# Second layer's W_in products by Strassen's rule (seven block products for eight) in chunks of 768 tokens

## The chip, the cores and the metric

The kernel runs on one core of a Trainium2 chip. The metric is the time of one execution on the device in microseconds (us); the median of three runs of the kernel before is 1091.63 us (1090.07 to 1092.5).

## The reference

Three stages follow one another: causal attention mixed with a memory read, a gated layer, and a second layer. Only the second layer's first product is computed in another way; all values are fp32, the weights arrive as float64 bit patterns.

```python
def _moe_ref(x, w_gate, w_val, w_out):      # x: 2304 x 512, d_ff = 1536
    gate = 1.0 / (1.0 + np.exp(-(x @ w_gate)))
    val = x @ w_val
    return (gate * val @ w_out).astype(np.float32)

def _moe2_ref(x, w_in, w_out):              # x: 2304 x 512, d_ff = 2048
    h = x @ w_in
    relu6 = np.clip(h + 3.0, 0.0, 6.0)
    g = h * relu6 / 6.0
    return (g @ w_out).astype(np.float32)
```

## The kernel before, in words

Every fp32 product is made of three matmuls on fp32r halves: each operand is split into a high part (a ScalarE copy that rounds) and a low part (a VectorE subtraction), and high·high, high·low and low·high are summed in PSUM (`mm3`, L181 to L185; `split`, L177). A weight is loaded as float64 bits into a staging tile `wst` (pool of 2), turned into fp32 by a chain of seven VectorE and two ScalarE operations (`convert`, L141 to L157, on 512 columns at a time in the later phases) and kept in one of 18 slots `wslot`.

Phase A (attention, with the first part of the gated layer as filler) ends near 418 us. Phase B (`phase_b`, L599) finishes the gated layer: five chunks of tokens, the last four of 468, and for each chunk and each block f of 128 hidden units `g1` (24 matmuls, then tanh on ScalarE, a product and the split on VectorE) and one item later `g2` (12 matmuls into the accumulators). Beside it VectorE and ScalarE convert weights ahead of time (`w_next`). When a chunk ends, VectorE adds the accumulators to `xp` (L643) and SyncE's queue writes the result to `x2` in DRAM.

Phase C (`phase_c`, L660) is the second layer: six chunks of 384 tokens by 16 blocks f. `g3` (L667) makes 12 matmuls of 384 columns for one block of h, then ScalarE and VectorE make `r` and split it into `hs`; `g4` (L684) of the item before makes 9 matmuls of 512 columns into three accumulators. All 16 blocks of both weights stay on the chip. In phases B and C the order on every engine is the scheduler's, which places each instruction by a simulated time; in phase A, and in the changed phase C, the order on TensorE is the program's.

Of the kernel before, what the change touches and what calls it, by code (L numbers as in the profile page):

```python
# [23 lines left out]
CB = 384  # L24
# [34 lines left out]
WB = 468  # L59

# [15 lines left out]
class Kernel:  # L76
# [64 lines left out]
    def convert(self, sl, st):  # L141
# [4 lines left out]


# [8 lines left out]
        nc.vector.tensor_tensor(hif, hif, lof, op=ALU.add)
        nc.vector.tensor_tensor(sl[:, 1], hif, sl[:, 0].bitcast(F32), op=ALU.subtract)  # L157

    def w_convert(self):
# [3 lines left out]
        keys, st, pool = self.wstaged.pop(0)  # L163
        sl = pool.tile([128, 2, len(keys), 512], F32R, name="wslot", tag="wslot")
# [293 lines left out]
    def phase_a(self):  # L458
# [99 lines left out]
        keys += [[(2, f, 0), (2, f, 1)] for f in range(FF2)]  # L558
# [40 lines left out]
    def phase_b(self):  # L599
# [7 lines left out]
        def g1(ci, t0, n, f, first, last):  # L607
            if first:
                st["xs"] = self.split_x(st["x"], n)
                nx = CHB[ci + 1] if ci + 1 < len(CHB) else None  # L610
                st["x"] = self.load_x(self.xd, *nx) if nx else self.load_x(self.x2, 0, CB)
# [36 lines left out]
        prev = None  # L648
# [8 lines left out]
        self.x_next = st["x"]  # L657


    def phase_c(self):  # L660
        nc = self.nc
        NTK = CB // 128
        NC = NT // CB
        work = [(c, f) for c in range(NC) for f in range(FF2)]
        st = {"x": self.x_next}

        def g3(c, f):  # L667
            if f == 0:
                st["xs"] = self.split_x(st["x"], CB)
                if c + 1 < NC:  # L670
                    st["x"] = self.load_x(self.x2, (c + 1) * CB, CB)
            w = self.weight(2, f, 0)
            ps = self.ps_g.tile([128, 512], F32, name="g", tag="g")
            for k in range(KT):
                cc = slice(128 * k, 128 * k + 128)
                self.mm3(ps[:, :CB], (w[:, 0, cc], w[:, 1, cc]), st["xs"][k], k == 0, k == KT - 1)
            r = self.br.tile([128, WB], F32, name="th", tag="th", bufs=2)
            gs = self.br.tile([128, 2, WB], F32R, name="hs", tag="hs", bufs=3)
            nc.scalar.activation(r[:, :CB], ps[:, :CB], AF.Relu, bias=self.three)  # L679
            nc.vector.scalar_tensor_tensor(r[:, :CB], r[:, :CB], 6.0, ps[:, :CB], op0=ALU.min, op1=ALU.mult)  # L680
            self.split(gs[:, 0, :CB], gs[:, 1, :CB], r[:, :CB], nc.scalar, nc.vector)
            return gs

        def g4(gs, c, f):  # L684
            w = self.weight(2, f, 1)
            if f == 0:
                st["acc"] = [self.ps_a.tile([128, 512], F32, name="acc", tag="acc") for _ in range(NTK)]
            for m in range(NTK):
                cc = slice(128 * m, 128 * m + 128)
                a = st["acc"][m]  # L690
                nc.tensor.matmul(a, gs[:, 0, cc], w[:, 0, :], start=(f == 0), stop=False)  # L691
                nc.tensor.matmul(a, gs[:, 0, cc], w[:, 1, :], start=False, stop=False)  # L692
                nc.tensor.matmul(a, gs[:, 1, cc], w[:, 0, :], start=False, stop=(f == FF2 - 1))  # L693
                if f == FF2 - 1:
                    o = self.br.tile([128, 512], F32, name="xp", tag="xp", bufs=4)
                    nc.scalar.activation(o, a, AF.Copy, scale=1.0 / 6.0)
                    r0 = c * CB + 128 * m
                    nc.sync.dma_start(self.out[r0 : r0 + 128, :], o)

        prev = None  # L700
        for item in work:
            gs = g3(*item)
            if prev:
                g4(*prev)
            prev = (gs, *item)
            self.w_next()
        g4(*prev)
# [64 lines left out]
```

## Time and profile before

| | |
|---|---|
| runs | 1092.5, 1090.07, 1091.63 us (median 1091.63) |
| profiled execution, span from first to last instruction | 1089.9 us |
| TensorE busy | 1059.1 us (97%) |
| VectorE busy / ScalarE busy | 610.6 us (56%) / 513.7 us (47%) |
| phase B, 418.3 to 686.0 us | VectorE 208.47 us, ScalarE 104.63 us of 267.70 |
| phase C, 685.8 to 1085.4 us | VectorE 130.14 us, ScalarE 124.48 us of 399.60 |

The profile is of one execution. A matmul's row shows a modelled end, so consecutive matmuls overlap in the rows: their rate is read from the starts. Busy shares do not tell what a stage waits for; the waits before an engine's instructions do. Of the 1091.63 us of the median, 1.7 lie outside the profiled span.

### The profile page before, as it was taken

To read this page: it belongs to the slowest core of one execution; us is meant where nothing else is said; L and a number is where in the kernel's file an instruction comes from. 1 tells how busy PE (TensorE), PEld (TensorE's weight loads), DVE (VectorE), ACT (ScalarE), POOL (GpSimd) and SP (SyncE) were. 2 spreads that over 40 slices of the span, in tenths; PEclk is the share of its full clock that TensorE was granted. 3 is DMA by queue.
4 is the path that set the end of the run, shared out by engine and by line. 5 is a ranking of instruction groups with operands and counts; after the bars stand their busy time and mean duration, and the time that the engine had idled before them with its cause. 6 is when DMAs were issued, how large, how long until landed. Compare 5 with 4: busy or idle time off the path is not lost.

```text
span 1089.9 us, 16041 instructions
## 1 busy us (share of the span) xinstructions
PE 1059.1 (97%) x5968; PEld 915.3 (84%) x5968; DVE 610.6 (56%) x1484; ACT 513.7 (47%) x1123; POOL 59.6 (5%) x90
## 2 busy tenths in 40 slices
PE   5789999999999999999999999999999999999998
PEld 3458778878878899999888888999999989999997
DVE  7999885453455358888987158923232232322322
ACT  5989885566546644345433134423233232332322
POOL 3212211100110000000000000000000000000000
PEclk9879999999999999999999999999999999999999
DMA  6755642424242134335353142301001010000000
GB/s 215 217 176 171 205 124 73 134 83 121 63 121 78 63 126 131 116 116 181 124 176 103 43 157 99 103 1 58 1 19 40 1 58 1 30 29 1 30 1 30
DMA packets 56303, 98.55 MB, mean 90 GB/s; under 512 B 7328, under 2 KB 40608, under 8 KB 56224
## 3 DMA queue, kind: packets, MB, share of 16 engines
q1 hardware_dynamic: 56224, 97.52, 27.9%
q8 instruction: 47, 0.77, 0.3%
q14 instruction: 32, 0.26, 0.1%
HBM read 79.51 MB, written 17.99 MB: 89 GB/s over the span
## 4 chain that ended last, share of the span: by engine, by line
PE 90%; DVE 4%; DMA 2%; ACT 2%; issue 1%; SPq 1%; POOL 0%; ACTq 0%
PE g L185 12%; PE g L184 12%; PE g L183 12%; PE acc L691 6%; PE acc L692 6%; PE acc L693 6%; PE m L183 6%; PE m L184 5%; PE m L185 5%; PE t L352 4%; PE pv L376 4%; PE s L294 4%; PE acc L183 3%; PE acc L185 3%; PE acc L184 3%; DMA aux<-in_aux 2%
## 5 line engine op out<-in xcount | busy, mean ns | idle before, releaser
L184 PE MATMUL g<-xs,wslot 128*128 128x384 f32 (+2 forms) x672 | 235.4, 351 | 0.0
L185 PE MATMUL g<-xs,wslot 128*128 128x384 f32 (+2 forms) x672 | 235.1, 351 | 0.0
L183 PE MATMUL g<-xs,wslot 128*128 128x384 f32 (+2 forms) x672 | 231.2, 351 | 0.0
L680 DVE SCALAR_TENSOR_TENSOR th<-th,g 128x384 f32<-128x384 f32 x96 | 53.2, 554 | 220.1 <-ACT th L679 219.8
L679 ACT ACTIVATE th<-g,three 128x384 f32<-128x384 f32 x96 | 55.8, 582 | 219.9 <-PE g L185 219.1
L184 PEld LDWEIGHTS g<-xs,wslot 128*128 128x128 f32 x672 | 126.1, 188 | 9.2
L183 PEld LDWEIGHTS g<-xs,wslot 128*128 128x128 f32 x672 | 126.0, 188 | 8.8
L185 PEld LDWEIGHTS g<-xs,wslot 128*128 128x128 f32 x672 | 126.1, 188 | 6.8
L178 ACT CAST hs<-th 128x384 fp32r<-128x384 f32 (+2 forms) x132 | 70.0, 530 | 92.9 <-DVE th L680 49.6
L691 PE MATMUL acc<-wslot,hs 128*128 128x512 f32 x288 | 113.7, 395 | 0.0
L692 PE MATMUL acc<-wslot,hs 128*128 128x512 f32 x288 | 113.5, 394 | 0.0
L693 PE MATMUL acc<-wslot,hs 128*128 128x512 f32 x288 | 109.2, 394 | 0.0
L179 DVE TENSOR_TENSOR hs<-th,hs 128x384 fp32r<-128x384 f32 (+2 forms) x132 | 76.1, 577 | 50.0 <-ACT hs L178 49.4
L312 ACT ACTIVATE P<-P,m 128x192 f32<-128x192 f32 (+4 forms) x144 | 84.1, 586 | 30.1 <-DVE m L274 28.8
L183 PE MATMUL m<-xs,wslot 128*128 128x312 f32 x288 | 93.7, 325 | 0.0
L184 PE MATMUL m<-xs,wslot 128*128 128x312 f32 x288 | 88.1, 306 | 0.0
L185 PE MATMUL m<-xs,wslot 128*128 128x312 f32 x288 | 87.9, 305 | 0.0
L294 PE MATMUL s<-qk 64*128 64x320 f32 (+3 forms) x320 | 70.5, 502 | 15.4 <-DMA qk<-in_qk 12.4
L352 PEld LDWEIGHTS t<-ident,P 128*128 128x128 f32 x464 | 56.6, 150 | 25.9 <-issue 15.0
L352 PE MATMUL t<-ident,P 128*128 128x128 f32 x464 | 71.5, 295 | 6.3 <-POOL P L327 3.6
L354 ACT COPY T<-t 128x512 f32<-128x512 f32 (+2 forms) x128 | 65.7, 541 | 14.3 <-PE t L352 14.3
L274 DVE CUSTOM_DVE_ANT_0 P<-s,mask 128x320 f32<-128x320 f32 (+3 forms) x144 | 62.5, 451 | 14.6 <-PE s L294 14.3
(78 smaller groups left out, 1752.7 us busy)
## 6 DMA issues: line engine op xcount, KB each, us to landing
wst<-in_wm SPq DMA_DIRECT2D x68, 512.0 KB, 4.3
qk<-in_qk SPq DMA_DIRECT2D x32, 160.0 KB, 2.3
aux<-in_aux SPq DMA_DIRECT2D x16, 320.0 KB, 3.4
qk<-in_qk SPq DMA_DIRECT2D x16, 288.0 KB, 3.0
x<-x SPq DMA_DIRECT2D x6, 768.0 KB, 4.5
out<-xp SPq DMA_DIRECT2D x18, 256.0 KB, 2.2
xc<-xd SPq DMA_DIRECT2D x24, 156.0 KB, 2.2
x2p<-xp SPq DMA_DIRECT2D x24, 156.0 KB, 1.8
```

The lines of the kernel that those rows point to most:

```text
L178: (ehi.copy if ehi is self.nc.scalar else ehi.tensor_copy)(hi, src)
L179: elo.tensor_tensor(lo, src, hi.bitcast(F32), op=ALU.subtract)
L183: nc.tensor.matmul(out, w[0], x[0], start=first, stop=False)
L184: nc.tensor.matmul(out, w[0], x[1], start=False, stop=False)
L185: nc.tensor.matmul(out, w[1], x[0], start=False, stop=last)
L294: nc.tensor.matmul(ps[:, : e - a], qk[rows, 0, q0 : q0 + 128], qk[rows, 1, a:e], start=True, stop=True)
L312: self.nc.scalar.activation(x, x, AF.Exp, bias=vs["m", rg][:, r : r + 1], scale=-1.0, accum_out=vs["l", rg][:, r : r + 1])
L352: nc.tensor.transpose(ps[:, 128 * n : 128 * n + 128], self.row(v, rg, r, 128 * j, 128 * j + 128), self.ident)
L354: nc.scalar.copy(pr["T", rg][:, 512 * k : 512 * k + c], ps[:, :c])
L691: nc.tensor.matmul(a, gs[:, 0, cc], w[:, 0, :], start=(f == 0), stop=False)
L692: nc.tensor.matmul(a, gs[:, 0, cc], w[:, 1, :], start=False, stop=False)
L693: nc.tensor.matmul(a, gs[:, 1, cc], w[:, 0, :], start=False, stop=(f == FF2 - 1))
```

## The change

Phase C works on chunks of 768 tokens and pairs of blocks f: the 2 by 2 by 2 block product of W_in's pair (two halves of the 512 inputs, two blocks of 128 units) with the chunk's activations (two halves of inputs, two halves of 384 tokens) is made by the Strassen-Winograd rule, that is seven products of 6 matmuls (of 384 columns) in place of eight. The sums of weights (`s`) are made on VectorE when a pair is converted, the sums of activations (`xt`, and in place in `xh`) on GpSimd, and the sums of products partly by accumulating in the same PSUM bank after a copy was taken (`m1`, `u2`, `u4`) and partly on VectorE (`c11`, `c22`, `c21`). The converted pairs no longer fit on the chip: each is written to `wd` in DRAM, and a ring of three pairs (nine slots) is refilled from there in phase C, where the chunks visit the pairs forth and back. All 16 conversions of the second layer fall into phase B. The matmuls of W_out (36 per pair of blocks) are let in between the products, five at a time, one step late.

```diff
+HC = 384
+NPAIR = FF2 // 2
+CSEQ = [(c, j if c % 2 == 0 else NPAIR - 1 - j) for c in range(NT // (2 * HC)) for j in range(NPAIR)]
+RING = 3
...
+    def convert_pair(self, j, up, st):
...
+        for i in range(2):
+            for _ in self.value(st[:, i : i + 1]):
+                pass
+        f = st.bitcast(F32)
+        v, s = f[:, :, :, 1], f[:, :, :, 0]
+        h0, h1 = slice(0, 256), slice(256, 512)
+        nc.vector.tensor_tensor(s[:, 0, h0], v[:, 1, h0], v[:, 1, h1], op=ALU.add)
+        nc.vector.tensor_tensor(s[:, 1, h0], v[:, 0, h0], v[:, 1, h0], op=ALU.subtract)
+        nc.vector.tensor_tensor(s[:, 0, h1], s[:, 0, h0], v[:, 0, h0], op=ALU.subtract)
+        nc.vector.tensor_tensor(s[:, 1, h1], v[:, 0, h1], s[:, 0, h1], op=ALU.subtract)
...
+            nc.scalar.copy(hi, src)
+            nc.vector.tensor_tensor(lo, src, hi.bitcast(F32), op=ALU.subtract)
+        nc.sync.dma_start(self.wd[j, 0], sa.bitcast(F32).rearrange("p a b c -> p (a b c)"))
+        nc.sync.dma_start(self.wd[j, 1, :, :1536], sb.bitcast(F32).rearrange("p a b c -> p (a b c)"))
...
-            for _ in range(2 - i % 2 if i < 12 else i % 2 if i < 30 else 1):
+            goal = min(2 * i + 2, 4) + (max(i - 1, 0) * 2 * NPAIR + 26) // 27
+            while done < min(goal, 4 + 2 * NPAIR):
                 self.w_next()
+                done += 1
+            left = len(work) - 1 - i
+            if left == 5:
+                self.c_load(0)
+            if left == 4:
+                self.c_sums()
+                order = self.c_order()
+            for _ in range({4: 2, 3: 2, 2: 1, 1: 2}.get(left, 0)):
+                self.c_block(*order.pop(0))
...
+    def c_load(self, c):
...
+            pool, tag = (self.bx, "x") if g == 0 else (self.stage, "wst")
+            t = pool.tile([128, KT, HC], F32, name="xh", tag=tag)
...
+        self.xt = self.stage.tile([128, 2, 2, HC], F32, name="xt", tag="wst")
...
+    def c_sums(self):
+        x0, x1 = self.xh
+        sub = lambda o, a, b: self.nc.gpsimd.tensor_tensor(o, a, b, op=ALU.subtract)
+        sub(self.xt[:, 0], x1[:, 0:2], x0[:, 0:2])
+        sub(self.xt[:, 1], x1[:, 2:4], self.xt[:, 0])
+        sub(x1[:, 0:2], x1[:, 2:4], x1[:, 0:2])
...
+        for s, (c, j) in enumerate(seq):
...
+            product(a, wa, 0, x["b11"], True, True)
+            m1 = sums("m1")
+            nc.scalar.copy(m1, a[:, :HC])
+            advance()
+            pump(5)
+            b = self.ps_g.tile([128, 512], F32, name="pb", tag="g")
+            product(b, wa, 1, x["b21"], True, True)
+            c11 = sums("c11")
+            add(c11, b[:, :HC], m1)
...
+            product(a, ws, 1, x["t2"], False, True)
+            u2 = sums("u2")
+            nc.scalar.copy(u2, a[:, :HC])
+            gated(c, 0, 0, c11)
...
+            product(b, ws, 2, x["t3"], True, True)
...
+            product(a, ws, 0, x["t1"], False, True)
+            u4 = sums("u4")
+            nc.scalar.copy(u4, a[:, :HC])
+            c22 = sums("c22")
+            add(c22, b[:, :HC], u4)
...
+            product(a, ws, 3, x["b22"], False, True)
+            gated(c, 0, 1, a[:, :HC])
+            gated(c, 1, 1, c22)
...
+            product(b, wa, 2, x["t4"], False, True)
+            c21 = sums("c21")
+            add(c21, b[:, :HC], u2)
+            gated(c, 1, 0, c21)
...
+            pump(36)
+            if s - 1 in swap:
+                self.c_fetch(swap[s - 1], "o")
+            if s in swap:
+                self.c_fetch(swap[s], "sa")
+            stream = second(s, dict(self.hs), w["o"])
```

`c_block` splits one 768-column block of activations into a slot of the seven that the gated layer's weights leave (`xq`); `advance` does one of them for the next chunk after each product of a chunk's last step; `gated` is the old ScalarE and VectorE work on h, once per quarter (four per step); `pump(n)` issues n of the 36 matmuls of W_out. Names and lines below: before, L149 to L157 conversion, L623/L643 product and result of phase B, L680 product of phase C; after, L152 to L164 the same conversion, L674/L694, L800 for the same three, L229 the split's subtraction, L851 the sums of products, L866/L877/L887 the copies.

**TensorE in the middle of phase C**, before: `g` are the products with W_in, `acc` those with W_out.

```order
L185 MATMUL g<-xs_7146,wslot 128x384
L183 MATMUL g<-xs_7149,wslot 128x384
L184 MATMUL g<-xs_7149,wslot 128x384
L185 MATMUL g<-xs_7149,wslot 128x384
L693 MATMUL acc<-wslot,hs 128x512 x3
L183 MATMUL g<-xs_7152,wslot 128x384
L184 MATMUL g<-xs_7152,wslot 128x384
```

After, products 5 to 7 of a step and the W_out matmuls let in behind each (`pa`, `pb` are the banks of the products):

```order
L787 MATMUL pa<-xq,wslot 128x384 x6
L822 MATMUL acc<-wslot,hs 128x512 x5
L787 MATMUL pa<-xq,wslot 128x384 x6
L822 MATMUL acc<-wslot,hs 128x512 x5
L787 MATMUL pb<-xq,wslot 128x384 x6
L822 MATMUL acc<-wslot,hs 128x512 x6
```

The free mix of two kinds became a fixed alternation, in which `pa` is copied (`u4`) and then added to with five matmuls between.

**VectorE where phase B meets phase C**, before (`xp` is the gated layer's result, `wst`/`wf`/`wslot` are conversion):

```order
L157 TENSOR_TENSOR wslot<-wst,wslot 128x512
L150 TENSOR_SCALAR wf<-wf 128x512
L151 SCALAR_TENSOR_TENSOR wst<-wst,wf 128x512
L643 SCALAR_TENSOR_TENSOR xp<-acc,xp 128x468
L680 SCALAR_TENSOR_TENSOR th<-th,g 128x384
L153 TENSOR_SCALAR wf<-wst 128x512
L643 SCALAR_TENSOR_TENSOR xp<-acc,xp 128x468 x3
L155 SCALAR_TENSOR_TENSOR wst<-wst,wf 128x512
```

After, the same place:

```order
L158 TENSOR_TENSOR wst<-wst 128x512
L694 SCALAR_TENSOR_TENSOR xp<-acc,xp 128x468 x2
L164 TENSOR_TENSOR wslot<-wst,wslot 128x512
L694 SCALAR_TENSOR_TENSOR xp<-acc,xp 128x468 x2
L851 TENSOR_TENSOR c_7278<-pb,m_7269 128x384
L800 SCALAR_TENSOR_TENSOR r<-r,c_7278 128x384
L229 TENSOR_TENSOR xq<-xt,xq 128x768
L229 TENSOR_TENSOR xq<-xh,xq 128x768
```

The last operation of the last conversion (L164) now stands between the gated layer's last results, and the splits of five activation blocks (three of them on sums) stand behind the first step's own work.

**ScalarE in phase C's first step**, after (nothing stood in its place before):

```order
L866 COPY m_7269<-pa 128x384
L799 ACTIVATE r<-c_7278,three 128x384
L228 CAST xq<-xt 128x768
L228 CAST xq<-xh 128x768
L228 CAST xq<-xt 128x768
L228 CAST xq<-xh 128x768
L228 CAST hs<-r 128x384
L228 CAST xq<-xh 128x768
L877 COPY u_7286<-pa 128x384
L887 COPY u_7307<-pa 128x384
```

The copy `u2` (L877), after which `pa` may be added to again, stands behind all five splits, the last of which needs GpSimd's fourth subtraction. In its order TensorE comes to the first two products of phase C (`b11`, `b21`) before the gated layer's last 12 matmuls, and to the third (`t2`) directly after them.

## Rows read from the trace of the kernel before

**Rows 1.** The page's busy times (engine, us, share, instructions).

```profile
PE 1059.1 (97%) x5968; PEld 915.3 (84%) x5968; DVE 610.6 (56%) x1484; ACT 513.7 (47%) x1123; POOL 59.6 (5%) x90
```

**Rows 2.** Windows of phase B and phase C: stretch, length, busy us by engine, clock, DMA.

```profile
418.30:686.00 267.70, 267.70 (x1298) 242.75 (x1297) 208.47 (x383) 104.63 (x178) 0.00 (x0) 1.00 0.37 124
685.80:1085.40 399.60, 399.54 (x1997) 360.50 (x1995) 130.14 (x241) 124.48 (x234) 0.00 (x0) 1.00 0.07 23
```

**Rows 3.** Timeline of TensorE in phase C: start, us, instruction.

```profile
896.07 0.40 PE L692 MATMUL acc<-wslot,hs 128*128 128x512 f32 x1
...
898.41 0.39 PE L693 MATMUL acc<-wslot,hs 128*128 128x512 f32 x1
...
903.16 0.34 PE L183 MATMUL g<-xs,wslot 128*128 128x384 f32 x1
...
905.78 0.34 PE L183 MATMUL g<-xs,wslot 128*128 128x384 f32 x1
```

**Rows 4.** Groups by line and shape: busy us, mean ns of one.

```profile
L679 ACT ACTIVATE th<-g,three 128x384 f32<-128x384 f32 x96 | 55.8, 582 | 219.9 <-PE g L185 219.1 <-DVE hs L179 0.6
...
L179 DVE TENSOR_TENSOR hs<-th,hs 128x384 fp32r<-128x384 f32 x96 | 53.5, 558 | 47.0 <-ACT hs L178 46.4
L680 DVE SCALAR_TENSOR_TENSOR th<-th,g 128x384 f32<-128x384 f32 x96 | 53.2, 554 | 220.1 <-ACT th L679 219.8
...
L179 DVE TENSOR_TENSOR hs<-th,hs 128x468 fp32r<-128x468 f32 x24 | 15.4, 640 | 2.6 <-ACT hs L178 2.6
...
L157 DVE TENSOR_TENSOR wslot<-wst,wslot 128x1024 fp32r<-128x1024 f32 x9 | 11.1, 1232 | 0.0
...
L249 DVE SCALAR_TENSOR_TENSOR ph<-aux,phw 128x320 f32<-128x320 f32 x16 | 8.3, 519 | 3.9 <-ACT phw L248 3.7
```

**Rows 5.** Timeline of VectorE in phase B: start, us, instruction, idle before it.

```profile
480.22 0.60 DVE L623 SCALAR_TENSOR_TENSOR th<-th,g 128x432 f32<-128x432 f32 x1 [0.25 <-PE g L185]
...
519.54 0.42 DVE L149 TENSOR_SCALAR wf<-wf 128x512 f32<-128x512 f32 x1
...
523.55 0.43 DVE L149 TENSOR_SCALAR wf<-wf 128x512 f32<-128x512 f32 x1
...
608.82 0.64 DVE L623 SCALAR_TENSOR_TENSOR th<-th,g 128x468 f32<-128x468 f32 x1 [5.72 <-PE g L185]
...
616.46 0.64 DVE L623 SCALAR_TENSOR_TENSOR th<-th,g 128x468 f32<-128x468 f32 x1 [5.71 <-PE g L185]
```

**Rows 6.** Timeline near 22 us: VectorE and GpSimd (POOL) beside each other.

```profile
21.38 1.19 DVE L156 TENSOR_TENSOR wst<-wst 128x1024 f32<-128x1024 f32 x1
...
21.54 1.60 POOL L327 TENSOR_TENSOR P<-ph,nr 128x320 f32<-128x320 f32 x1 [3.52 <-DVE nr L259]
...
22.48 1.01 DVE L249 SCALAR_TENSOR_TENSOR ph<-aux,phw 128x320 f32<-128x320 f32 x1
...
23.85 0.73 POOL L255 TENSOR_TENSOR phw<-ph,zz 128x256 f32<-128x256 f32 x1
```

**Rows 7.** Timeline of GpSimd: an operation of the same line, undisturbed.

```profile
171.60 0.72 POOL L327 TENSOR_TENSOR P<-ph,nr 128x320 f32<-128x320 f32 x1 [1.66 <-PE m L185]
```

**Rows 8.** Windows of phase A around idle stretches of TensorE (the ninth column is the granted clock).

```profile
24.50:26.00 1.50, 0.00 (x0) 0.00 (x0) 1.50 (x4) 0.70 (x4) 0.08 (x1) 1.00 0.82 249
26.50:29.50 3.00, 3.00 (x15) 2.32 (x14) 3.00 (x14) 1.89 (x6) 0.00 (x0) 0.50 0.65 199
30.00:32.00 2.00, 2.00 (x18) 1.05 (x16) 1.92 (x6) 2.00 (x9) 0.00 (x0) 1.00 1.01 307
...
51.00:63.00 12.00, 11.38 (x38) 7.31 (x38) 11.99 (x28) 12.00 (x26) 3.04 (x4) 0.50 0.47 148
```

**Rows 9.** Timeline at the end of phase C: the last split and its matmul.

```profile
1082.43 0.51 ACT L178 CAST hs<-th 128x384 fp32r<-128x384 f32 x1 [0.62 <-DVE th L680]
...
1082.99 0.19 PEld L691 LDWEIGHTS acc<-wslot,hs 128*128 128x128 f32 x1 [0.22 <-ACT hs L178]
```

**Rows 10.** DMA issues: the loads of the second layer's activations, KB each, us to landing.

```profile
x<-x SPq DMA_DIRECT2D x6, 768.0 KB, 4.5
```

More of the change, by code (lines that the diff above doesn't have):

```diff
@@ L23 @@
 CA = 312
-CB = 384
 BIG = 1.0e30
@@ L163, in w_convert @@
         keys, st, pool = self.wstaged.pop(0)
+        if keys[0][0] == 2:
+            self.convert_pair(keys[0][1] // 2, keys[0][2] == 0, st)
+            return
         sl = pool.tile([128, 2, len(keys), 512], F32R, name="wslot", tag="wslot")
@@ L557, in phase_a @@
             keys += [[(1, f, 0), (1, f, 1)], [(1, f + 1, 0), (1, f + 1, 1)], [(1, f, 2), (1, f + 1, 2)]]
-        keys += [[(2, f, 0), (2, f, 1)] for f in range(FF2)]
+        self.ring = {}
+        for j in [*range(RING, NPAIR), *range(RING)]:
+            keys += [[(2, 2 * j, which), (2, 2 * j + 1, which)] for which in range(2)]
         self.plan_weights(keys, [])
@@ L609, in g1 @@
                 st["xs"] = self.split_x(st["x"], n)
[L610 to L611 removed]
+                if ci + 1 < len(CHB):
+                    st["x"] = self.load_x(self.xd, *CHB[ci + 1])
             p = []
@@ L646, in g2 @@
                     nc.sync.dma_start(self.x2[m, :, t0 : t0 + n], xp)
-        prev = None
+        prev, done = None, 0
+        order = []
         for i, item in enumerate(work):
@@ L653, in phase_b @@
             prev = (hs, *item)
-            for _ in range(2 - i % 2 if i < 12 else i % 2 if i < 30 else 1):
+            goal = min(2 * i + 2, 4) + (max(i - 1, 0) * 2 * NPAIR + 26) // 27
+            while done < min(goal, 4 + 2 * NPAIR):
                 self.w_next()
-        g2(*prev)
-        self.x_next = st["x"]
-    def phase_c(self):
[L661 to L674, printed above, removed]
-                cc = slice(128 * k, 128 * k + 128)
[L676 to L697, printed above, removed]
-                    nc.sync.dma_start(self.out[r0 : r0 + 128, :], o)
[L700 to L707, printed above, removed]
@@ new lines, in phase_b @@
+                done += 1
[7 more added lines that the diff above has]
+                self.c_block(*order.pop(0))
+        g2(*prev)
+        self.b_ctx.close()
+    def c_load(self, c):
+        self.xh = []
+        for g in range(2):
+            pool, tag = (self.bx, "x") if g == 0 else (self.stage, "wst")
+            t = pool.tile([128, KT, HC], F32, name="xh", tag=tag)
+            t0 = (2 * c + g) * HC
+            self.nc.sync.dma_start(t, self.x2[:, :, t0 : t0 + HC].rearrange("k p t -> p k t"))
+            self.xh.append(t)
+        self.xt = self.stage.tile([128, 2, 2, HC], F32, name="xt", tag="wst")
+        self.xs = {}
@@ new lines, in c_sums, with c_order @@
+    def c_sums(self):
[4 more added lines that the diff above has]
+        sub(x1[:, 0:2], x1[:, 2:4], x1[:, 0:2])
+    def c_order(self):
+        x0, x1 = self.xh
+        return [
+            ("b11", x0[:, 0:2]),
+            ("b21", x0[:, 2:4]),
+            ("t2", self.xt[:, 1]),
+            ("t3", x1[:, 0:2]),
+            ("t1", self.xt[:, 0]),
+            ("b22", x1[:, 2:4]),
+            ("t4", x0[:, 2:4]),
+        ]
@@ new lines, in c_block, with c_fetch @@
+    def c_block(self, name, src):
+        if name == "t4":
+            self.nc.gpsimd.tensor_tensor(src, src, self.xt[:, 1], op=ALU.subtract)
+        t = self.wpool2.tile([128, 2, 2, HC], F32R, name="xq", tag="wslot")
+        self.split(t[:, 0], t[:, 1], src, self.nc.scalar, self.nc.vector)
+        self.xs[name] = t
+    def c_fetch(self, j, names):
+        for name in names:
+            n, w, i = {"s": (4, 256, 0), "a": (3, 256, 1), "o": (2, 512, 2)}[name]
+            t = self.wpool.tile([128, 2, n, w], F32R, name="wslot", tag="wslot")
+            self.nc.sync.dma_start(t.bitcast(F32).rearrange("p a b c -> p (a b c)"), self.wd[j, i, :, : 2 * n * w])
+            self.ring[j][name] = t
```

137 lines of the change are left out of this document (131 added, 6 removed).

## Prediction

> **What bounds the kernel now.** I read the busy times first: TensorE 97% of the span [rows 1]. Then the stages by windows: in phase B TensorE has work for all of 267.70 us, VectorE for 208; in phase C TensorE for 399.54 of 399.60 us, VectorE and ScalarE for a third, DMA 0.07 [rows 2]. So in phase C the time is a count of matmuls times their spacing, and what is left off TensorE there comes off the end, as long as the rest keeps up. The spacing is read from starts: 15 steps between 903.16 and 905.78 give 0.175 us for 384 columns, 10 steps between 896.07 and 898.41 give 0.234 us for 512 [rows 3]. Check: 96 items of 12 and 9 such matmuls make 403 us against 399.6 seen [rows 2, 3], 1% too much.
>
> **1. Matmuls saved.** Before, phase C makes 6 x 16 x 12 = 1152 matmuls of 384 columns; after, 3 x 8 x 42 = 1008. W_out keeps its 864. 144 x 0.175 = 25.2 us, less 1% by the check: **-25.0 us**. (The Trainium skill, "TensorE: Matmul & The Clock Gate", section "Back-to-back issue gap", gives a warm gap of N/2.4 + 2.5 ns, an estimate of 162.5 ns here; 144 of them would be 23.4 us. The spacing in the trace is 7% longer, and the trace decides.)
>
> **2. A step in the middle of phase C: nothing.** 42 x 0.175 + 36 x 0.234 = 15.8 us of TensorE [rows 3]. Per step VectorE has 4 products, 4 split subtractions and 3 sums, 11 x 0.555 = 6.1 us; ScalarE 4 x 0.58 (L679), 4 casts of 0.51 and 3 copies, about 6 us [rows 4, 9]. Both are under half busy. The tightest wait is product 6, which adds to the bank that `u4` is copied from after product 5: in between lie five matmuls, 1.17 us. The copy needs the 0.16 us that the last matmul outlasts its slot, 0.1 to start, 0.51 to run and 0.05 until TensorE follows [rows 3, 9]: 0.85 us. It fits by 0.3. The other copies and sums have two products and ten matmuls of cover or more. The refills are 2.75 MB per step at most, used two steps (31 us) after they are asked for; a 768 KB load lands in 4.5 us [rows 10], so four of them, one behind the other, need 18.
>
> **3. Phase B: VectorE fills up.** One conversion of 512 columns repeats after 4.01 us [rows 5]. A W_out pair is two: 8.0. A W_in pair is two without their last operation (0.61), four sums of 256 columns (about 0.42 each, by L179's 0.56 at 384 and 0.64 at 468 [rows 4]) and splits of 1024, 512 and 256 columns (1.23, 0.68, 0.42): 6.8 + 1.7 + 2.3 = 10.8. Eight pairs: 150 us. From 480.2 us, where the first pair begins, VectorE also has 26 items x 2 x 0.64, 16 input splits and 16 results of 0.64 and two blocks of 768 columns (about 0.95): 33 + 20 + 2. Sum 205 us of durations; TensorE needs from 480.2 to 686: 206 us [rows 2, 5]. Rows that run back to back overlap by some 0.09 us, so the true need is near 195: about 5% to spare. A late `hs` has a cover of 24 matmuls, 24 x 0.212 = 5.1 us (36 in 7.64 us [rows 5]), and the lumps (two conversions between two products) stay under that. I take **+1.5 us**, from 0 to 6.
>
> **4. From B to C: the gap.** Let T be the end of the last `g1`. TensorE then makes 12 matmuls (2.5 us), `b11` and `b21` (2.1) and the last 12 (2.5): it is free at T + 7.2 and comes to `t2`. `t2` is the second GpSimd sum, and `xt` takes the staging tile of the last conversion. In VectorE's order L164 of that conversion stands behind two results `xp`, the second of which needs the second of four accumulators (T + 6.4), so L164 ends at T + 7.9. GpSimd has 0.73 us for 256 columns [rows 6], 0.72 for 320 [rows 7]: 1.7 to 2.2 for 768, I take 1.85. Two sums: T + 11.7. ScalarE's cast of 768 (about 0.9, from 0.51 at 384 [rows 9]) ends at T + 12.6. Until then TensorE stands still for over 5 us, and the second matmul of `t2` needs VectorE's subtraction.
>
> Here VectorE and GpSimd meet. Near 22 us a GpSimd operation that takes 0.72 alone [rows 7] shows 1.60 beside a VectorE operation on two inputs, ending 0.6 after it, and the next VectorE operation on two inputs shows 1.01 where its mean is 0.52 [rows 4, 6]. So they exclude each other, and I let them alternate: `t2`'s low part ends at T + 15.0, `t3`'s at 17.8, `t1`'s at 18.7, `b22`'s at 19.5, `t4`'s at 20.9. ScalarE comes to `u2` only behind all five casts, at T + 18.1, done 18.7. Product 3 ends at T + 15.9, product 4 at 18.7, product 5 at 19.8, product 6 (after `u4`) at 21.6, product 7 at 22.7. Without a wait product 7 would end at 7.2 + 5 x 1.05 = 12.4: 10.3 us lost; without the exclusion 9.4. (The Trainium skill, "SBUF — State Buffer", section "SBUF: two separate sides", calls this an exclusive lock on a shared pair of ports, held for the whole instruction; the trace agrees at 21.54 us with 1.60 against 0.72. It speaks against putting the sums on GpSimd.)
>
> And the clock: after 1.5 us without a matmul the granted clock went to 0.50, was back at 30 us after some 3 us of dense work [rows 8], and in another place stayed at 0.50 for the 12 us from 51 to 63 while TensorE worked with breaks. A standstill of 5 us will bring it to 1.2 GHz here. Products 3 and 4 wait anyway; if two of the rest run at half speed it costs 2.1 us more. **+12.5 us**; from 8 (no exclusion, clock unharmed, faster casts) to 18 (half speed into the second step).
>
> **5. The two changes of chunk: +4 us.** In a chunk's last step seven 768-column splits come on top: ScalarE 6 + 7 x 0.9 = 12.3, VectorE 6.1 + 7 x 0.95 = 12.8 of 15.8 us. The last block's cast stands ahead of the last quarter's work and has to wait for product 7; the chain `c21`, relu, product, cast is then some 4.7 us after product 7, while the new stream asks for it after 6 + 6 + 3 matmuls, 3.2 us. I take 2 us each (GpSimd's fourth sum falls in there too), from 0.8 to 4.
>
> **6. The end: +0.5 us.** After the last product the same chain (five operations of 0.51 to 0.58 and the steps between, to the cast 2.6 us) has nine matmuls, 2.1 us, of cover. The last copy and write are as before.
>
> **Sum:** -25.0 + 1.5 + 12.5 + 4 + 0.5 = -6.5. The span goes from 1089.9 to 1083.4; 1.7 us lie outside it, so **1085 us**. The ends of the terms: 1076 and 1097.
>
> **Rivals.**
> - *The gap stays small: 1070 us.* If L164 and the sums are done well before TensorE asks (conversions that run ahead of the scheduler's picture), part 4 shrinks to the 2 to 3 us that `m1`, `u2` and `u4` cost without cover, and part 5 to 1: 1091.6 - 25 + 3.4. For it: VectorE idles some 5.7 us per item around 612 us before [rows 5], so it can run ahead. Against it: L164 stands in the order behind results that need the last 12 matmuls, whatever VectorE's speed.
> - *VectorE becomes the bound in phase B: 1096 us, slower.* Place: the conversions between 490 and 686 us. If a pair's conversion takes 12 instead of 10.8 us, because its splits wait for ScalarE's casts and its writes to DRAM hold slots, the need passes 206 us; at 5% more it is 205, at 10% 215, and from there each us is one at the end. 10 us more than the forecast. For it: 195 of 206 is the fullest stretch of the kernel. Against it: VectorE at 208 of 267.70 us left TensorE full throughout phase B [rows 2], and its overlap in back-to-back rows is not yet spent.
> - *The cover inside a step fails: 1097 us, slower.* The 0.3 us of part 2 is thin. If ScalarE is in another operation (0.58) when product 5 ends, each of 24 steps loses up to 0.5: 12 us. It decides from 0.27 us per step on, 6.5 in all.
> - *The exclusion of GpSimd and VectorE costs more: 1090 us, no change.* With every sum of a chunk change paying a two-input VectorE operation on both sides (four sums, 4 x 0.6 per change), part 5 rises to 9. This is the page's rule taken at its worst; the rows show both sides stretched once.
> - *The change does not do what it says:* the order has 42 and 36 matmuls in a step, so this is left 0.02, at 1092.
>
> **How the numbers follow.** Forecast 0.50 (own range 1079 to 1090), small gap 0.15, VectorE bound 0.13, steps 0.12, exclusion 0.08, nothing 0.02. A measurement of this kernel can tell some 0.2% from no change, 2.2 us: faster is below 1089.4. That holds for nearly all of the forecast, all of the small gap and a little of the exclusion: 0.66. Same: half of the exclusion, the last case, the edges of the others: 0.10. Slower: 0.24. The range 1074 to 1096 leaves out most of the small-gap case and the upper halves of the two slow ones, about 0.2.
>
> **What would show it.** Phase C's middle steps at 15.6 to 15.8 us with no idle TensorE, at `pa` above all; 1872 matmuls in it; one standstill of TensorE of 5 to 7 us near 686 us in front of `t2`, then waits for `t3` and for `u2`, and the clock at 0.5 behind it; GpSimd sums of 1.8 us, some stretched to near 3; two small stalls at the chunk changes. TensorE idle between 490 and 680 us would mean that VectorE is the bound; a wait at `pa` in every step, that part 2 is wrong; a sum `xt` that ends before T + 9, that part 4 is.

## The result and the profile after

The changed kernel takes 1079.76 us (median of 4 runs, 1078.99 to 1081.34) against 1091.99 us (4 runs beside it, 1090.07 to 1092.5): a ratio of 0.9893, 95% interval 0.9879 to 0.9907. The profiled execution has a span of 1078.2 us, with 1.7 outside it.

The page's busy times of the changed kernel, against [rows 1]:

```profile
PE 1037.6 (96%) x5824; PEld 890.3 (83%) x5824; DVE 684.2 (63%) x1602; ACT 551.5 (51%) x1191; POOL 83.2 (8%) x102
```

TensorE has 144 matmuls less, VectorE 73.6 us more. Then its windows, columns as in [rows 2]: phase B to the last `g1`, the rest of the gated layer with the first two products, products 3 to 7 of the first step, and the rest.

```profile
418.00:676.56 258.56, 258.56 (x1250) 234.17 (x1250) 231.72 (x434) 110.64 (x186) 0.00 (x0) 1.00 0.58 207
676.56:683.72 7.16, 7.16 (x37) 6.39 (x35) 6.26 (x12) 1.71 (x4) 0.00 (x0) 1.00 0.99 348
683.72:700.19 16.47, 8.96 (x31) 7.56 (x31) 12.67 (x14) 6.60 (x11) 8.19 (x4) 0.69 0.57 199
700.19:1078.20 378.01, 372.12 (x1831) 331.73 (x1830) 160.87 (x283) 148.21 (x281) 15.86 (x8) 1.00 0.36 133
```

VectorE is busy for 231.72 of 258.56 us of phase B, and TensorE still never stops in it. All of TensorE's waits from 400 us on (engine, operation waiting, what it waited for, us in total, times, longest):

```profile
PE pa L787 <- ACT xq L228: 5.4, 1, 5.4
PE acc L822 <- ACT hs L228: 2.2, 3, 0.9
PE pa L787 <- DVE xq L229: 1.3, 1, 1.3
PE pa L787 <- ACT u L887: 0.6, 1, 0.6
PE pb L787 <- DVE xq L229: 0.2, 1, 0.2
```

Four of the five lines are one place, products 3 to 6 of the first step; the three waits at `acc` are the two changes of chunk and the end. The place, in TensorE's timeline (the first row is the gated layer's last matmul, the last one the next step's first product):

```profile
683.51 0.38 PE L235 MATMUL acc<-hs,wslot 128*128 128x468 f32 x1
689.27 0.69 PE L787 MATMUL pa<-xq,wslot 128*128 128x384 f32 x1 [5.38 <-ACT xq L228]
691.30 1.97 PE L787 MATMUL pa<-xq,wslot 128*128 128x384 f32 x5 [1.34 <-DVE xq L229]
693.07 0.52 PE L787 MATMUL pb<-xq,wslot 128*128 128x384 f32 x1
693.81 1.97 PE L787 MATMUL pb<-xq,wslot 128*128 128x384 f32 x5 [0.22 <-DVE xq L229]
695.58 1.82 PE L787 MATMUL pa<-xq,wslot 128*128 128x384 f32 x6
697.97 1.33 PE L787 MATMUL pa<-xq,wslot 128*128 128x384 f32 x6 [0.57 <-ACT u L887]
699.13 1.22 PE L787 MATMUL pb<-xq,wslot 128*128 128x384 f32 x6
700.19 1.22 PE L787 MATMUL pa<-xq,wslot 128*128 128x384 f32 x6
```

Products 3 to 7 need 5 x 1.05 us; they take from 683.72 to 700.19, 16.47 us. 11.2 us are lost there. What they wait for, by the other engines' rows (ScalarE's and VectorE's `xq` are the split of `t2`):

```profile
676.83 1.17 SPq L728 DMA_DIRECT2D xh<-x  x1
...
683.76 0.68 DVE L164 TENSOR_TENSOR wslot<-wst,wslot 128x512 fp32r<-128x512 f32 x1
684.67 1.81 POOL L735 TENSOR_TENSOR xt<-xh 128x768 f32<-128x768 f32 x1 [319.82 <-DVE wslot L164]
686.55 1.80 POOL L735 TENSOR_TENSOR xt<-xh,xt 128x768 f32<-128x768 f32 x1
688.39 0.83 ACT L228 CAST xq<-xt 128x768 fp32r<-128x768 f32 x1 [1.72 <-POOL xt L735]
689.25 2.00 DVE L229 TENSOR_TENSOR xq<-xt,xq 128x768 fp32r<-128x768 f32 x1 [0.48 <-ACT xq L228]
...
702.90 1.85 POOL L735 TENSOR_TENSOR xt<-xh 128x768 f32<-128x768 f32 x1 [9.96 <-DMA xh<-x]
```

The last `g1` ends at T = 676.56, so L164 ends at T + 7.9, the second sum at T + 11.8, the cast at T + 12.7 and the subtraction at T + 14.7: the chain of the prediction, link by link. The first sum had a second condition that the prediction leaves out: the load of the second half of `xh`, asked for at 676.83 us (first row), took 7.3 us by the tile's view and landed at 684.2, T + 7.6, only 0.3 us ahead of L164's end. So an earlier L164 alone could have gained no more than that 0.3 us. The last row is the first sum for the next chunk, made in the second step.

A step in the middle, from one first product to the next: 843.23 - 827.46 = 15.77 us.

```profile
827.46 1.22 PE L787 MATMUL pa<-xq,wslot 128*128 128x384 f32 x6
...
843.23 1.22 PE L787 MATMUL pa<-xq,wslot 128*128 128x384 f32 x6
```

### The profile page after: what moved, and what is told of

Same layout as the page of the kernel before. It is cut to its first block, busy times and chain, and to the rows that moved or that the text cites. A ratio compares the mean times of both kernels' runs of the same rounds, so it can differ in the third digit from the quotient of the medians.

```text
span 1078.2 us, 16086 instructions
## 1 busy us (share of the span) xinstructions
PE 1037.6 (96%) x5824; PEld 890.3 (83%) x5824; DVE 684.2 (63%) x1602; ACT 551.5 (51%) x1191; POOL 83.2 (8%) x102
## 4 chain that ended last, share of the span: by engine, by line
PE 85%; DVE 7%; ACT 3%; DMA 2%; issue 1%; POOL 1%; SPq 0%; POOLq 0%; ACTq 0%
PE acc L822 18%; PE pa L787 9%; PE pb L787 7%; PE g L235 6%; PE g L233 6%; PE g L234 6%; PE m L233 5%; PE m L234 5%; PE m L235 5%; PE pv L426 4%; PE t L402 4%; PE s L344 3%; PE acc L233 3%; PE acc L235 3%; PE acc L234 3%; DMA aux<-in_aux 2%
## 5 line engine op out<-in xcount | busy, mean ns | idle before, releaser
L822 PE MATMUL acc<-wslot,hs 128*128 128x512 f32 x864 | 227.8, 395 | 2.2 <-ACT hs L228 2.2
L822 PEld LDWEIGHTS acc<-wslot,hs 128*128 128x128 f32 x864 | 159.5, 188 | 27.7 <-ACT hs L228 3.5
L787 PE MATMUL pa<-xq,wslot 128*128 128x384 f32 x576 | 119.3, 342 | 7.3 <-ACT xq L228 5.4
L787 PEld LDWEIGHTS pa<-xq,wslot 128*128 128x128 f32 x576 | 105.1, 190 | 16.6 <-ACT xq L228 5.8
L235 PE MATMUL g<-xs,wslot 128*128 128x468 f32 (+1 forms) x288 | 106.1, 369 | 0.0
L234 PE MATMUL g<-xs,wslot 128*128 128x468 f32 (+1 forms) x288 | 105.6, 369 | 0.0
L233 PE MATMUL g<-xs,wslot 128*128 128x468 f32 (+1 forms) x288 | 103.9, 369 | 0.0
L787 PE MATMUL pb<-xq,wslot 128*128 128x384 f32 x432 | 89.1, 341 | 0.2 <-DVE xq L229 0.2
L344 PE MATMUL s<-qk 64*128 64x320 f32 (+3 forms) x320 | 70.8, 502 | 14.3 <-DMA qk<-in_qk 11.8
L787 PEld LDWEIGHTS pb<-xq,wslot 128*128 128x128 f32 x432 | 78.6, 189 | 7.0 <-DVE xq L229 0.7
L851 DVE TENSOR_TENSOR c<-pb,u 128x384 f32<-128x384 f32 x48 | 26.6, 555 | 88.1 <-ACT u L887 87.1
L799 ACT ACTIVATE r<-c,three 128x384 f32<-128x384 f32 x72 | 44.2, 614 | 61.9 <-DVE c L851 61.9
L229 DVE TENSOR_TENSOR hs<-r,hs 128x384 fp32r<-128x384 f32 x96 | 55.9, 586 | 26.3 <-ACT hs L228 24.8
L426 PE MATMUL pv<-T,aux 128*64 128x256 f32 (+2 forms) x512 | 63.4, 377 | 4.5 <-ACT T L404 4.5
```

What stands on the lines that cost most here:

```text
L229: elo.tensor_tensor(lo, src, hi.bitcast(F32), op=ALU.subtract)
L233: nc.tensor.matmul(out, w[0], x[0], start=first, stop=False)
L234: nc.tensor.matmul(out, w[0], x[1], start=False, stop=False)
L235: nc.tensor.matmul(out, w[1], x[0], start=False, stop=last)
L344: nc.tensor.matmul(ps[:, : e - a], qk[rows, 0, q0 : q0 + 128], qk[rows, 1, a:e], start=True, stop=True)
L426: nc.tensor.matmul(ps[rows, o : o + w], pr["v"][:, j, rows], T[:, c : c + w], start=(n == 0), stop=(n == last), skip_group_check=True,)
```

## The experiments

In each, times are medians; beside them stands what TensorE's rows show of the profiled execution. For the first step I use one measure, from the first product of phase C to the first of the second step: 21.1 us in the changed kernel (679.09 to 700.19), 9.9 if nothing waited (two products 2.1, twelve matmuls 2.55, five products 5.25). It does not carry the scatter of phase A, whose last matmul started between 416.1 and 419.7 us in these executions. But it has a scatter of its own: experiments 2 and 8 leave the first step as it is, and it took 20.2 us there (677.09 to 697.25) and 20.6 (679.67 to 700.26), because the clock came back earlier (experiment 6). A difference of 1 us in it shows little by itself.

**1. Eight products again.**

```diff
             product(b, ws, 2, x["t3"], True, True)
+            product(b, ws, 2, x["t3"], True, True)
```

> The product with t3 is made twice, so that each of the 24 steps has eight products of 6 matmuls again; nothing else changes. Theory (matmuls times their spacing set every step): 144 x 0.1767 = 25.4 us more, about 1105.2 us, a step of 15.77 + 1.06 = 16.83 us. Rival (the chain of copies, sums and splits, or the refills, sets the step, and the saved matmuls are partly hidden): clearly less than 25 us more, down to nothing.

1105.57 us (1105.26 to 1106.05): 25.8 more. The step is 16.83 us long, from 888.15 to 904.98:

```profile
888.15 1.22 PE L787 MATMUL pa<-xq,wslot 128*128 128x384 f32 x6
...
904.98 1.22 PE L787 MATMUL pa<-xq,wslot 128*128 128x384 f32 x6
```

TensorE's waits are the same five lines. So each saved matmul came off the end, and with eight products the new scheme is 1.4% slower than the kernel before (ratio 1.0136, 1.0121 to 1.0151): everything else in the change costs.

**2. The cover of the copy `u4`.**

```diff
             add(c22, b[:, :HC], u4)
             advance()
-            pump(5)
+            pump(2)
...
             gated(c, 1, 1, c22)
             advance()
-            pump(5)
+            pump(8)
```

> Between products 5 and 6 stand two matmuls of W_out in place of five, the other three behind product 6. Theory (the copy u4 needs 0.85 us from the last slot of product 5 to the first of product 6, two matmuls cover 0.46): a wait of 0.39 us at pa in 23 of 24 steps, 9 us more, about 1088.7 us. Rival (the copy is quicker than I added up, the cover was never tight): no change, 1079.8. Rival (ScalarE is often in another operation when product 5 ends): 0.6 us or more in each step, 1094 or more.

1089.2 us (1086.13 to 1090.51), 9.4 more. Products 5 and 6 of a step, and product 5 of the next:

```profile
884.90 1.22 PE L787 MATMUL pa<-xq,wslot 128*128 128x384 f32 x6
885.96 0.63 PE L822 MATMUL acc<-wslot,hs 128*128 128x512 f32 x2
886.74 1.33 PE L787 MATMUL pa<-xq,wslot 128*128 128x384 f32 x6 [0.16 <-ACT u L887]
...
901.11 1.22 PE L787 MATMUL pa<-xq,wslot 128*128 128x384 f32 x6
```

The step is 16.21 us, 0.44 longer. Product 6 starts 0.78 us after product 5's last slot (two matmuls of 0.232 would be 0.46) and runs 0.1 longer. So the copy costs about 0.88 us between the two products, 0.85 as added up; five matmuls, 1.16 us, cover it, and three, 0.70, would not by this sum (no run has three). The 0.16 us of idle in the row understates the wait, since the matmuls ahead have modelled ends.

**3. The sums earlier, on GpSimd.**

```diff
-            pool, tag = (self.bx, "x") if g == 0 else (self.stage, "wst")
+            pool, tag = (self.bx, "x") if g == 0 else (self.bx, "xh1")
...
-            if left == 5:
+            if left == 7:
                 self.c_load(0)
-            if left == 4:
+            if left == 6:
                 self.c_sums()
```

> The second half of the first chunk's activations gets a tile of its own (room from one th, one hs, one r less and a shared tile for c11 and c21), so that the sums xt take the staging tile that comes free one conversion earlier, and the load and the sums are asked for two items earlier. GpSimd still makes the sums. Theory (the break before the third product comes from the staging tile of the last conversion, then two GpSimd sums): the sums run from about 677 us instead of 684.7, the third product starts with no wait, the clock stays up, and of 11.2 us lost there some 3 are left (2 to 5): about 1071.5 us. Rival (VectorE's load at the end of phase B makes the break, whatever the tile): 7 us or more are left, 1075.5 or more. Rival (GpSimd's sums now stretch VectorE's operations for the gated layer's last item): 4 us come back at the last hs, 1075 or more.

1079.09 us, ratio 0.989 (0.9874 to 0.9907): nothing gained. My theory fell and the third reading held. The sums did run 7 us earlier, beside VectorE:

```profile
677.44 2.10 POOL L735 TENSOR_TENSOR xt<-xh 128x768 f32<-128x768 f32 x1 [311.85 <-DVE wslot L202]
679.61 1.91 POOL L735 TENSOR_TENSOR xt<-xh,xt 128x768 f32<-128x768 f32 x1
681.48 2.27 POOL L735 TENSOR_TENSOR xh<-xh 128x768 f32<-128x768 f32 x1
683.72 1.98 POOL L754 TENSOR_TENSOR xh<-xh,xt 128x768 f32<-128x768 f32 x1
```

```profile
677.74 0.63 DVE L674 SCALAR_TENSOR_TENSOR th<-th,g 128x468 f32<-128x468 f32 x1
678.29 1.53 DVE L152 TENSOR_SCALAR wf<-wf 128x512 f32<-128x512 f32 x1
679.74 2.33 DVE L164 TENSOR_TENSOR wslot<-wst,wslot 128x512 fp32r<-128x512 f32 x1
682.00 2.04 DVE L153 TENSOR_SCALAR wf<-wf 128x512 int32<-128x512 int32 x1
683.96 2.24 DVE L229 TENSOR_TENSOR hs<-th,hs 128x468 fp32r<-128x468 f32 x1
```

One VectorE operation per GpSimd sum: each ends 0.3 to 0.6 us after a sum does. Four operations that take 0.42, 0.69, 0.42 and 0.64 us elsewhere filled 7.9 us, from 678.29 to 686.20; only L674, in the first row, did not stretch. The last of them is the low part of the gated layer's last `hs`, and TensorE waited 3.2 us for it (686.25). The clock fell with it (granted 0.50 from 688 to 697 us): products 3 to 5 take 2.1 to 2.2 us each (the first from 690.87 to 692.95), twice their usual time, some 3 us more in all. First step: 20.1 us (679.94 to 700.03).

**4. The sums earlier, on VectorE.** As 3, and

```diff
-        sub = lambda o, a, b: self.nc.gpsimd.tensor_tensor(o, a, b, op=ALU.subtract)
+        sub = lambda o, a, b: self.nc.vector.tensor_tensor(o, a, b, op=ALU.subtract)
...
-            self.nc.gpsimd.tensor_tensor(src, src, self.xt[:, 1], op=ALU.subtract)
+            self.nc.vector.tensor_tensor(src, src, self.xt[:, 1], op=ALU.subtract)
```

> As the run before this one, but all sums of activations are made on VectorE. Theory (VectorE and GpSimd exclude each other, so a sum on GpSimd costs VectorE as much as its own sum would): VectorE has four operations of 0.96 us more but none is stretched beside GpSimd; 2 to 4 us of the 11.2 are left, 1071 us, 1 to 3 us less than with GpSimd. Rival (no exclusion, VectorE is simply full): the four sums push the last items' split back by up to 3.8 us, 1 to 3 us more than with GpSimd.

1073.67 us (1073.33 to 1074.64), ratio 0.9844 (0.983 to 0.9859). Better than expected against GpSimd (5.4 us where 1 to 3 were said), less good in all (1071). The first step takes 13.3 us (680.61 to 693.95): 7.8 less than in the changed kernel, with 3.4 left. Of the 7.8 us, 1.0 comes back in the second step, 16.7 us long, where TensorE waits for an `hs` whose subtraction stands behind operations of the last conversion. The granted clock stayed at 1.00 here, so some 3 of the 5.4 us are the clock that experiment 3 lost by its wait. To make room, 3 and 4 also have one buffer less of `th`, `hs` and `r` and one tile for `c11` and `c21`; no run shows what this costs by itself, but both have it, so it is not in the 5.4 us.

**5. On VectorE, but not earlier.** The second diff of 4 alone.

> The sums of activations are made on VectorE, with the tiles and the order of loads as in the changed kernel. Theory (in the break the sums stand behind the last conversion whatever engine makes them; VectorE gains the exclusion but has c11, a product and the results xp ahead of them): the second half of the third product starts between 690 and 692 us as before, the later subtractions follow at 0.87 us each and are not stretched, so 0.5 to 3 us less, 1077 to 1079.5 us. Rival (GpSimd and its exclusion alone make the break): the 7 us that the early sums on VectorE gave come back here too, 1073 to 1075. Rival (at the changes of chunk the four sums on VectorE cost more than GpSimd's): waits at hs of more than 2.2 us, 1081 or more.

1080.45 us (1079.53 to 1080.98), ratio 0.9899 (0.9883 to 0.9916): no gain by time, a little above the range given. The first step is 20.0 us (680.64 to 700.68), 1.1 less. In the profiled execution this is made up by phase A, which ended 1.55 us later, and by the second step, 0.35 us longer than usual. That the 1.1 us are not the clock's return alone shows at the start of product 5, before the clock is back in either: 18.0 us from the end of the last `g1`, against 19.0 in the changed kernel (19.0 also in experiment 8, 18.7 in 2). So neither half does it alone: late sums cost the break whatever makes them, early ones on GpSimd cost it through VectorE.

**6. The clock in the break.**

```diff
+            if s == 0:
+                d = self.ps_a.tile([128, 512], F32, name="pd", tag="acc")
+                for _ in range(7):
+                    product(d, wa, 0, x["b11"], True, True)
             product(a, ws, 1, x["t2"], False, True)
+            if s == 0:
+                product(d, wa, 0, x["b11"], True, True)
```

> Throwaway products keep TensorE busy in the break: seven (42 matmuls, 7.4 us) ahead of the product with t2 and one between it and the product with t3, into a bank that nothing reads; the order on VectorE stays as it is. Theory (in the break the chain of sums, casts and subtractions sets the time, and the lower clock costs only what products 5 to 7 lose at it): granted clock 1.0 throughout, product 4 still waits for its subtraction at 693.8 us, products 5 to 7 end some 1.3 us earlier, 1078.4 us. Rival (the clock makes all of the 3.7 us by which the loss exceeds the idle time): 1076. Rival (the throwaway matmuls only push the products back): no change or slower.

1078.5 us (1078.37 to 1078.92). Windows of the changed kernel in the break (the ninth column is the granted clock), then of this run:

```profile
683.72:689.00 5.28, 0.17 (x1) 0.00 (x0) 4.37 (x6) 1.23 (x2) 4.26 (x3) 0.78 0.93 357
689.00:691.30 2.30, 0.69 (x1) 0.29 (x1) 2.00 (x1) 1.05 (x3) 2.30 (x2) 0.50 0.17 58
691.30:693.00 1.70, 1.70 (x5) 1.70 (x6) 1.67 (x1) 1.70 (x3) 1.64 (x1) 0.50 0.00 0
695.60:697.00 1.40, 1.40 (x6) 1.40 (x5) 1.23 (x2) 0.00 (x0) 0.00 (x0) 0.54 0.67 134
```

```profile
683.40:690.70 7.30, 7.30 (x43) 7.27 (x43) 6.13 (x7) 1.85 (x3) 6.25 (x4) 1.00 0.74 279
690.70:695.00 4.30, 4.11 (x23) 3.48 (x22) 4.21 (x4) 3.43 (x6) 2.08 (x1) 1.00 0.00 0
695.00:698.60 3.60, 3.03 (x17) 2.71 (x16) 2.37 (x5) 1.31 (x3) 0.00 (x0) 1.00 0.79 231
```

The clock stayed at 2.4 GHz and the first step took 19.8 us (678.80 to 698.63), 1.3 less, as expected. So of the 3.7 us by which the loss exceeds the idle time in the changed kernel's execution, 2.4 would have been waited anyway. Against experiments 2 and 8, whose first step is the changed kernel's, the gain is only 0.3 and 0.8 us: when the clock came back differs from one execution to the next. This is the window of experiment 2 that lies where the changed kernel's last one above does, 19.0 us behind the last `g1`:

```profile
693.59:694.99 1.40, 0.91 (x6) 0.59 (x4) 1.23 (x2) 0.45 (x1) 0.00 (x0) 1.00 0.66 149
```

So the lower clock cost 0.3 to 1.3 us in these executions.

**7. More for VectorE in phase B.** The four sums of weights in `convert_pair` stand in a loop that runs twice.

```diff
-        nc.vector.tensor_tensor(s[:, 0, h0], v[:, 1, h0], v[:, 1, h1], op=ALU.add)
...
+        for _ in range(2):
+            nc.vector.tensor_tensor(s[:, 0, h0], v[:, 1, h0], v[:, 1, h1], op=ALU.add)
...
```

> Each of the four sums of weights of a pair is made twice (the same values), 8 x 4 x 0.42 = 13.4 us more for VectorE in phase B. VectorE shows 231.7 us busy of 258.6 there. Theory (VectorE is not the bound in phase B, but its work is in program order and what does not fit lands at the end of phase B, ahead of the sums of activations): no wait of TensorE before its last g1, and the break before the third product grows from 11.2 us to some 17 to 25, so 1086 to 1093 us. Rival (VectorE has 27 us of room and takes it in): within 2 us of 1079.8. Rival (VectorE is the bound in phase B): TensorE waits for hs between 480 and 676 us, 1093 with these waits summing to some 13 us.

1100.59 us (1100.43 to 1101.55), 20.8 more; my range missed it by 7.6. TensorE waited 0.6 us for one `hs` in phase B and 25.2 in the break:

```profile
701.22 0.69 DVE L164 TENSOR_TENSOR wslot<-wst,wslot 128x512 fp32r<-128x512 f32 x1
710.75 1.69 DVE L230 TENSOR_TENSOR xq<-xt,xq 128x768 fp32r<-128x768 f32 x1 [8.84 <-ACT xq L229]
```

```profile
706.16 1.80 POOL L736 TENSOR_TENSOR xt<-xh 128x768 f32<-128x768 f32 x1 [340.59 <-DMA xh<-x]
```

The last conversion ends at 701.9 us in place of 684.4: 17.5 later, the work added (13.4 us by the lengths of its rows, some 11 by their starts) and the first step's own operations that now stand ahead of it. And the sums no longer wait for L164 but for the load of `xh` into the other staging tile, which in the changed kernel landed just ahead of L164: 4 us more. So VectorE's idle time was no room: it is busy for 228.8 of 259.4 us of phase B here, no more than in the changed kernel, and what was added lies behind it. Of its 27 us of idle time in phase B in the changed kernel 14.1 are waits of L674 for `g1` (23 waits, by the waits view): the next operation in VectorE's order needs matmuls that TensorE has not made yet, and later work stands behind it. In this run VectorE also waits 9.6 us for `wf` (3.1 in the changed kernel), which ScalarE makes from a staging tile once its load has landed. How much the order and how much the two staging tiles held the work back, the run does not separate.

**8. The order of the last step's accumulators.**

```diff
-            order = [(f, t) for t in range(6) for f in range(2)] if last else [(f, t) for f in range(2) for t in range(6)]
+            order = [(f, t) for t in (3, 4, 5, 0, 1, 2) for f in range(2)] if last else [(f, t) for f in range(2) for t in range(6)]
```

> In a chunk's last step the six accumulators are made in the order 3, 4, 5, 0, 1, 2 in place of 0 to 5, so that the quarter made last is asked for after 18 matmuls and not after 3; nothing else changes. Theory (the three waits for hs, 2.2 us in all, two at the changes of chunk and one at the end, are the chain from product 7 to the cast with three to nine matmuls of cover): all three go, 1077.6 us. Rival (the waits come from ScalarE and VectorE being full in a chunk's last step): they stay, at the new place, 1079.8.

1077.27 us (1076.82 to 1077.89), 2.5 less; the line `acc L822 <- ACT hs` is gone from the waits. The two steps at the changes of chunk are 15.77 us long in place of 16.90, and the last step to the end of the span is 1.0 us shorter, 3.2 us by the traces. The three waits were a chain with too little cover and nothing else.

**9, 10. The last pair's conversions in phase C.** Both have 8's order; 10 also has 4's second diff.

```diff
-        self.plan_weights(keys, [])
+        self.late = keys[-2:]
+        self.plan_weights(keys[:-2], [])
...
-            while done < min(goal, 4 + 2 * NPAIR):
+            while done < min(goal, 2 + 2 * NPAIR):
...
-            if s % NPAIR == 1 and c + 1 < len(seq) // NPAIR:
+            if s % NPAIR == 3 and c + 1 < len(seq) // NPAIR:
                 self.c_load(c + 1)
...
+            if s == 0:
+                self.wkeys = self.late
+                self.w_load()
+                self.w_load()
+            if s < 2:
+                self.w_convert()
```

> The order of the run before this one, and the last pair's two conversions are loaded and made in the first steps of phase C (the pair is used two steps later), so that the staging tiles are free for the activations some 18 us of VectorE work earlier; the next chunk's load is asked for two steps later. GpSimd still makes the sums. Theory (the break was the end of the conversions meeting the sums, and GpSimd's sums cost only where VectorE is asked for at once): the sums lie 10 us or more ahead of the last g1, the third product does not wait for them, 2 to 3 us of 11.2 are left (copies without cover), 1069 us. Rival (the conversions now collide with the first steps of phase C): waits at pa or hs of 5 us or more in steps 0 to 2, 1073 or more. Rival (the exclusion with GpSimd moves into the last items of phase B): TensorE waits 2 to 4 us for an hs there, 1072.

> As the run before this one with the sums of activations on VectorE. Theory: with the sums off the critical place it matters little which engine makes them, within 1.5 us of the run before, 1068 to 1070. Rival (GpSimd costs VectorE more than the sums themselves, also here): 2 to 4 us faster than the run before. Rival (VectorE is full): slower than the run before by 2 us or more.

With GpSimd's sums 1071.65 us (1070.02 to 1072.01), ratio 0.9811 (0.9794 to 0.9827); with VectorE's 1068.3 us (1067.77 to 1069.21), ratio 0.9785 (0.977 to 0.9799). In run 10 the sums are made 14 us ahead of the first product, and one wait is left after 400 us, for `u4`: ScalarE comes to this copy behind the relu of `c11`, and that sum stands on VectorE behind operations of the conversion and results `xp`:

```profile
665.68 0.96 DVE L736 TENSOR_TENSOR xt<-xh 128x768 f32<-128x768 f32 x1 [1.46 <-DMA xh<-x]
...
679.86 1.20 PE L788 MATMUL pa<-xq,wslot 128*128 128x384 f32 x6
...
689.55 1.33 PE L788 MATMUL pa<-xq,wslot 128*128 128x384 f32 x6 [1.61 <-ACT u L888]
...
691.91 1.22 PE L788 MATMUL pa<-xq,wslot 128*128 128x384 f32 x6
```

The first step takes 12.05 us. Against expectation GpSimd's sums cost 3.3 us more here too. In run 9 TensorE waits 2.5 us for `u2`, which stands on ScalarE behind a conversion operation that is some 5 us later than in run 10. The splits beside GpSimd are stretched again (subtractions of 1.72 and 2.07 us where 0.95 is usual), so the staging tile, its next load and the conversion all come later. In run 9's wait for `u2` the clock fell too (granted 0.59 from 692 to 695 us), and products 6 and 7 take 3.5 us where run 10 has 2.4. How much of the 3.3 us comes from the stretched splits and how much from the order, these two runs do not separate. Run 10 is the fastest version, and beats both kernels.

## Why the prediction was right, and where its sum was off

The forecast was 1085 us, 1079.76 were measured: 5.2 us less, inside the range but at the fast edge of the forecast's own one, 1079 to 1090. By its own steps:

- **1, matmuls saved (-25.0).** Run 1 gives -25.8 by the medians and 24 x 1.06 = -25.4 by the step. The 1% taken off by the check was a miscount: the window of [rows 2] has 1997 matmuls, phase C 2016. By the gap that the Trainium skill ("TensorE: Matmul & The Clock Gate", section "Back-to-back issue gap") gives for an isolated matmul, the estimate is 23.4 us for 144 matmuls, 2 us too short here.
- **2, a step costs nothing more.** 15.77 us, 15.8 said. Run 2 bears out the tightest place: 0.88 us needed (0.85 said), 1.16 there. The rival that the cover fails does not hold.
- **3, VectorE in phase B (+1.5).** No wait between 418 and 683 us, so 0. But the view behind it, 5% to spare, was wrong in kind: in run 7 phase B took in none of the work added. I looked for the cost as late `hs` in phase B; it shows at the end, where the last conversion meets the sums. The rival "VectorE becomes the bound" had the right engine and the wrong place.
- **4, the gap (+12.5).** 11.2. L164 at T + 7.9 (7.9 said), the second sum at 11.8 (11.7), the cast at 12.7 (12.6), the subtraction at 14.7 (15.0), product 7's end at 23.6 (22.7). The clock was put at 2.1 us and is 0.3 to 1.3 (runs 2, 6 and 8). The gap is mis-sized by little, but one link is missing from the sum: the load of `xh`, which landed at T + 7.6. It was there 0.3 us before L164 ended, so leaving it out did not change the number; that is luck. The rival that the gap stays small is out: that needed both the load and the last conversion's work out of the way, as runs 9 and 10 made it.
- **5 and 6, changes of chunk and end (+4.5).** 2.2 us of waits, 2.5 by the medians of run 8, 3.2 by its steps (1.1 for each change, 1.0 for the end). I priced each change at 2 us for GpSimd's fourth sum and full engines. The first three sums of the next chunk ran in the second step already (702.90 us, as soon as the load had landed), the fourth at 800.24 us, 10 us ahead of the next chunk's first product (810.56), and the wait is only the chain with three matmuls of cover.

-25.4 + 11.2 + 3.2 = -11.0. From the start of phase A's last matmul (418.9 us before, 418.1 after) to the end of the span the two profiled executions differ by the same 11.0 us. The spans differ by 11.7: phase A was 0.8 us shorter, which is inside its scatter. So of the 5.2 us 1.5 are step 3, 1.3 step 4, 1.3 steps 5 and 6 and 0.4 step 1, and the 0.7 left is scatter.

The rule of the Trainium skill ("SBUF — State Buffer", section "SBUF: two separate sides") that GpSimd and VectorE lock each other out of a shared pair of ports was given a small rival, 1090 us. As a mechanism the exclusion, with the clock that fell by its wait, is what decides between runs 3 and 4 (5.4 us); in the changed kernel itself, taking the sums off GpSimd gains about 1 us of the break (run 5), because there the chain waits for the conversion and the load first.

## What to carry to other kernels

Where an engine that feeds the bound one is busy for 90% of a stage, ask where its last operation ends and what stands behind it, not how much idle time it shows: here its work ran in order, and what was added came out at the seam to the next stage, as 20.8 us for 13.4 us of added rows. Move work across the seam into a stage where that engine is half idle; here this gave 5.6 us beyond the reordering of run 8 with the sums left on GpSimd, and 9.0 with the sums on VectorE as well, three quarters as much as the whole change. And a break must be taken apart in pairs of edits: of two causes in a row, removing either one alone gave about 1 us of the first step, both 7.8.

## What the runs showed of the hardware that was not expected

- GpSimd and VectorE alternated operation by operation in run 3: four VectorE operations filled 7.9 us beside four sums. There also operations with one tensor as input were held (L152 1.53 us, L153 2.04, usually 0.42), not only those with two; the product L674, which reads a PSUM bank and one tile, took its usual 0.63 us beside a sum. The Trainium skill ("SBUF — State Buffer", section "SBUF: two separate sides") names for the lock VectorE's operations with two SBUF inputs and those in a two-port mode; L674, L164 and L229 agree with it, and the mode of L152 and L153 no run here shows.
- TensorE's clock fell to 1.2 GHz within the 5.4 us of idle time, with the granted clock at 0.50 from 689.0 to 695.6 us although TensorE worked from 691.3 on, and it stayed at 2.4 GHz where throwaway matmuls filled the break. Behind the same break it came back at another place in experiment 2 (1.00 from 693.59 us, 19.0 us behind the last `g1`; 0.54 there in the changed kernel). Keeping it up was worth 0.3 to 1.3 us.
